# Sums of x in two tasks and two lanes, begun when the block's x is there

## The chip, the cores and the metric

The kernel runs on one core of a Trainium2 chip. The time is that of the device, in microseconds (us), from one execution of the program; three executions of the kernel before gave 2139.3, 2142.45 and 2143.07, a median of 2142.45. The profile is that of one more execution.

## What is computed

Three layers follow one another, all in 32 bits:

```
attention (4 batches, 8 heads, 576 tokens, head 64, 128 random features):
    phi(x) = exp(x @ omega.T - |x|^2/2 - max) / sqrt(128)
    out    = phi(q) (phi(k)^T v) / (phi(q) sum(phi(k)) + 1e-6)       -> x [2304, 512]
first layer (8 experts, w1[e] 512 x 1024, w2[e] 1024 x 512):
    P = exp(x @ w_gate - max); 8 times: rows /= sums, columns /= sums, *= 2304/8
    x = sum over e of P[:, e] * (relu(x @ w1[e]) @ w2[e])
second layer (w_in 512 x 2048, w_out 2048 x 512):
    out = (h * sigmoid(1.702 h)) @ w_out,   h = x @ w_in
```

## The kernel before

**Tiles.** Every 32-bit operand of a matmul is split into a high part (`..h`) and a rest (`..l`), and each product is three matmuls: high times high, high times low, low times high. The 2304 tokens are three blocks of 768 (`j` = 0, 1, 2). A block's x lies transposed in `blk_h[j]` and `blk_l[j]`: 4 k tiles of 128 of the 512 inner elements by 768 tokens. The 1024 or 2048 middle columns go in chunks of 256. One **visit** of the loop in `moe` is one chunk with one block (in the first expert partly half a block); there are 128 of them, numbered from 0. A visit has an up part (x times the chunk of the first weight, into `hh`, `hl`) and a down part of 36 matmuls (tile `py`, L892), whose results VectorE adds to the accumulators.

**Two ways up.** The first expert and the first chunk of the second layer (`ch` is `(E, 0)`) use `up`: 48 matmuls a visit (tile `ph`, L713). All other visits use `up_fast`: the 2 x 2 product of halves (two k halves, two token halves) is made with seven products in place of eight, 42 matmuls (L805), at the price of sums of weights and of x. Visits 0 to 19 are the first expert, 0 to 15 for blocks 0 and 1 (most of them beside attention), 16 to 19 for block 2. Visit 20 is the first with `up_fast`, block 0; 21 is block 1, 22 block 2. Visits 104, 105 and 106 are chunk `(E, 0)` of the second layer; 107, 108 and 109 are its first with `up_fast`.

**The sums of x.** With X[kh][i] for k half kh and token half i, `up_fast` wants s1 = X01 + X11, s2 = s1 - X00, s3 = X00 - X01 (tiles `th`, `tl`, high and low, index 0, 1, 2) and s4 = X10 - s2, which is written over X01 itself. For each of the two k tiles of a half (`kk`), `x_sums` (L729) issues two operations on VectorE and seven on GpSimd (`tt`, L738; names `t` and `u`), four casts to the high part on ScalarE (L761, L767, L772, L781) and four rests on VectorE (`lo`, L743). It is one generator per block: kk = 0 is issued wholly before kk = 1, with one `t` and one `u` from the pool of two buffers `t2`. s4 stands at the end of each kk, since X01 may be overwritten only when the `up` visits of the block are past (`free`).

**What sets the order.** The program is recorded in the order in which this code runs, and each engine executes its own instructions in that order. After each piece of a visit the loop at L1092 adds an estimate of its TensorE time to `now`, and calls `background()` (L958), which runs one step of one generator: a begun `spare` (the doubling of the second layer's weights from 64 bits, `double_piece`, L531), else the first of the deque `urgent` (the sums), else a new `spare`. `pool_done` (L102) holds a step back until `now` has passed the estimate `pool` of GpSimd's end. Every third piece also runs a step of `gates`, the eight row and column divisions (`sinkhorn`, L478: VectorE, then a matmul `pc`, L508, that TensorE runs in its place). A block's sums go into `urgent` when no `up` visit of the first layer needs the block any more (L1056), or, for the second layer, at the end of visits 102 to 104 (L1058). Before an `up_fast` visit, L1028 looks whether the block's sums are all issued; if not, `hurry` issues the rest at once, ahead of the visit.

**Others on GpSimd.** GpSimd also makes the sums of the weights of a chunk (`make_sums`, L628) and the low parts of the next chunk's first weight (`split`, L579, tiles `g0l`, `g1l`, `g2l`), which the first visit of that chunk reads.

## Time and profile before

| | |
|---|---|
| median of three runs | 2142.45 us |
| the profiled execution | 2136.16 us, span 2133.7 us |
| TensorE (PE) busy | 2090.6 us, 98% of the span |
| VectorE (DVE) busy | 1409.1 us, 66% |
| ScalarE (ACT) busy | 798.7 us, 37% |
| GpSimd (POOL) busy | 482.6 us, 23% |
| mean granted TensorE clock | 0.993 of full speed |

The span runs from the first to the last instruction; 2.5 us of the profiled execution lie outside it. Attention lasts until about 308 us of the span, the first layer until about 1723, the second to the end. PE is matmuls, PEld weight loads. A wait counts only on the engine that others wait for, here nearly always TensorE.

### The profile page before, as it was taken

The numbers are of one execution on the slowest core, as the hardware profiler recorded it, in microseconds if no ns is written. First come the engines' busy times: TensorE is split into PE (matmuls) and PEld (weight loads), VectorE is DVE, ScalarE is ACT, GpSimd is POOL, SyncE is SP. The second block draws the span as 40 slices with busy tenths as digits, with TensorE's granted clock in tenths as the row PEclk, the third lists the DMA queues.
The fourth block names the chain that finished last, engine by engine and source line by source line (L and its number), as shares of the span: only waits on it lengthen the run. The fifth ranks groups of instructions, "written<-read, shape, count | busy, mean of one in ns | idle before, by whom it ended". The sixth has DMA issues, their size and how long they took to land.

```text
span 2133.7 us, 29280 instructions
## 1 busy us (share of the span) xinstructions
PE 2090.6 (98%) x11040; PEld 1894.8 (89%) x11040; DVE 1409.1 (66%) x2630; ACT 798.7 (37%) x1770; POOL 482.6 (23%) x505
## 2 busy tenths in 40 slices
PE   8999999989999999999999999999999998799999
PEld 8999978878989999899999989999998997799987
DVE  7666547767666766766667676766555666566676
ACT  7655543532333323223332322333232354343443
POOL 3212224522121112212211221222111035311110
PEclk9999999999999999999999999999999999899999
DMA  8333211111112111111111111111000000000002
GB/s 164 86 80 90 70 52 48 40 37 46 45 42 59 51 50 44 49 45 42 57 53 50 43 50 45 43 57 33 20 20 20 20 20 20 20 21 20 20 21 89
DMA packets 147965, 100.54 MB, mean 47 GB/s; under 512 B 63600, under 2 KB 125040, under 8 KB 147824
## 3 DMA queue, kind: packets, MB, share of 16 engines
q1 hardware_dynamic: 147824, 98.68, 16.6%
q8 instruction: 86, 1.41, 0.3%
q14 instruction: 55, 0.45, 0.1%
HBM read 85.54 MB, written 13.11 MB: 46 GB/s over the span
## 4 chain that ended last, share of the span: by engine, by line
PE 92%; DVE 4%; ACT 2%; POOL 1%; issue 1%; DMA 0%; SPq 0%; ACTq 0%; POOLq 0%; DVEq 0%
PE py L892 45%; PE le L805 15%; PE ri L805 10%; PE ph L713 6%; PE pc L805 5%; PE pd L805 5%; PE num L304 2%; PE kv L274 1%; POOL u L738 1%; PE xt L342 1%; PE pj L240 1%; PE pj L242 1%; PE pj L241 1%; PE qt L297 1%; PE pt L215 1%
## 5 line engine op out<-in xcount | busy, mean ns | idle before, releaser
L892 PE MATMUL py<-w,hh 128*128 128x512 f32 x2880 | 895.6, 392 | 0.6 <-ACT hh L676 0.6
L892 PEld LDWEIGHTS py<-w,hh 128*128 128x128 f32 x2880 | 533.3, 188 | 104.7 <-ACT hh L676 1.9
L892 PE MATMUL py<-w,hl 128*128 128x512 f32 x1440 | 563.5, 391 | 0.0
L909 DVE SCALAR_TENSOR_TENSOR a<-py,lg,a 128x512 f32<-128x512 f32 x504 | 367.0, 747 | 132.7 <-PE py L892 132.4
L892 PEld LDWEIGHTS py<-w,hl 128*128 128x128 f32 x1440 | 270.2, 188 | 58.2 <-DVE hl L684 0.9
L823 ACT COPY m<-le 128x384 f32<-128x384 f32 x105 | 50.3, 479 | 528.5 <-PE le L805 528.4
L579 POOL TENSOR_TENSOR g0l<-w,g0h 128x768 fp32r<-128x768 f32 (+1 forms) x52 | 86.9, 1671 | 698.3 <-ACT g0h L578 679.8
L563 POOL TENSOR_TENSOR tmp<-tmp 128x256 f32<-128x256 f32 x64 | 47.3, 739 | 636.4 <-DVE tmp L560 346.5
L816 DVE TENSOR_TENSOR pc<-pc,m 128x384 f32<-128x384 f32 x105 | 59.5, 566 | 140.1 <-PE pc L805 140.0
L628 POOL TENSOR_TENSOR w<-w 128x256 f32<-128x256 f32 x140 | 108.0, 792 | 41.1 <-DMA w<-scr_in 22.1
L579 DVE TENSOR_TENSOR w<-r,w 128x512 fp32r<-128x512 f32 x104 | 75.8, 742 | 50.9 <-ACT w L578 50.9
L686 DVE SCALAR_TENSOR_TENSOR hl<-pc,hh 128x384 fp32r<-128x384 f32 x84 | 46.8, 558 | 90.8 <-ACT hh L678 89.2
L578 ACT CAST w<-r 128x512 fp32r<-128x512 f32 x104 | 63.6, 629 | 115.2 <-PE py L892 114.7
L837 ACT COPY u<-le 128x384 f32<-128x384 f32 x105 | 50.5, 481 | 137.7 <-PE le L805 137.7
L260 ACT ACTIVATE feat<-pj,nb 128x128 f32<-128x128 f32 x272 | 73.9, 386 | 68.2 <-DVE nb L256 61.5
L913 DVE TENSOR_TENSOR o<-py,o 128x512 f32<-128x512 f32 x126 | 84.3, 686 | 22.4 <-PE py L892 22.2
L816 DVE TENSOR_TENSOR le<-le,m 128x384 f32<-128x384 f32 x105 | 59.3, 565 | 45.7 <-ACT m L857 45.7
L805 PE MATMUL le<-th,g1h 128*128 128x384 f32 x210 | 73.1, 348 | 12.9 <-ACT m L823 12.9
L805 PE MATMUL ri<-th,g0h 128*128 128x384 f32 x210 | 72.2, 344 | 9.6 <-ACT th L761 9.6
L678 ACT ACTIVATE hh<-ri 128x384 fp32r<-128x384 f32 x84 | 41.2, 491 | 91.6 <-DVE ri L816 91.6
L805 PE MATMUL le<-tl,g1h 128*128 128x384 f32 x210 | 72.4, 345 | 0.0
L805 PE MATMUL ri<-tl,g0h 128*128 128x384 f32 x210 | 72.1, 344 | 0.2 <-DVE tl L743 0.2
(252 smaller groups left out, 4561.6 us busy)
## 6 DMA issues: line engine op xcount, KB each, us to landing
w<-in_moe_w_dram SPq DMA_DIRECT2D x176, 128.0 KB, 2.4
r<-in_moe_w_dram SPq DMA_DIRECT2D x44, 512.0 KB, 3.7
raw<-in_moe_w_in_dram SPq DMA_DIRECT2D x32, 256.0 KB, 3.0
raw<-in_moe_w_out_dram SPq DMA_DIRECT2D x32, 256.0 KB, 2.9
k<-in_k_dram SPq DMA_DIRECT2D x16, 256.0 KB, 4.2
v<-in_v_dram SPq DMA_DIRECT2D x16, 256.0 KB, 4.8
q<-in_q_dram SPq DMA_DIRECT2D x16, 256.0 KB, 4.6
scr_in<-tmp SPq DMA_DIRECT2D x32, 128.0 KB, 1.9
```

Of the source, the lines that this page charges most:

```text
L260: nc.scalar.activation(f[:, h, :], pvs[h // 4][:, h % 4, :], AF.Exp, bias=nb[:, h : h + 1])
L578: nc.scalar.copy(hi, r)
L579: eng.tensor_tensor(out=lo, in0=r, in1=hi.bitcast(F32), op=ALU.subtract)
L628: nc.gpsimd.tensor_tensor(out=r[:, o], in0=r[:, x], in1=r[:, y], op=ALU.subtract)
L713: nc.tensor.matmul(o, w[kk][a], x[j][:, 2 * kh + kk, th * Q : (th + 1) * Q], start=m == 0, stop=m == 3 * NK - 1,)
L805: nc.tensor.matmul(o, a[kk][x], b[kk][y], start=start and kk == 0 and n == 0, stop=kk == 1 and n == 2, skip_group_check=True,)
L816: nc.vector.tensor_tensor(out=o, in0=a, in1=b, op=ALU.add)
L823: nc.scalar.copy(m1, le)
L837: nc.scalar.copy(u2, le)
L892: nc.tensor.matmul(py[t], a[:, c], w, start=f == halves[0] and m == 0, stop=f == halves[1] and m == 2,)
L909: nc.vector.scalar_tensor_tensor(out=o, in0=py, scalar=pg[:, n, e : e + 1], in1=o, op0=ALU.mult, op1=ALU.add)
L913: nc.vector.tensor_tensor(out=o, in0=py, in1=o, op=ALU.add)
```

## The change

The sums become two tasks for each block, and each task is two generators, one for each `kk`. `x_sums` makes s1, s3 and s2 (five operations on GpSimd for each kk), and `x_sum4` makes s4 from X10 and the finished s2, high and low part apart (three on GpSimd). `urgent` becomes a list of two deques (lanes), and `background` runs a step of both. Lane 1 takes its `t` and `u` from two more buffers, `t3`, in the phase's own pool. `x_sums` of all three blocks goes into the lanes when attention is over, `x_sum4` of blocks 0 and 1 behind it, that of block 2 at the end of visit 19, and those of the second layer at the end of visits 104, 105 and 106. `free` and `used` go. In the order, L735 and L739 of the new program are what L738 and L743 were.

```diff
--- before.py
+++ after.py
@@ -726,7 +726,22 @@
 
     sums_done = set()
 
-    def x_sums(key, xh, xl, free):
+    def new_temp(lane, name):
+        if lane == 0:
+            return tm2([P, Q], F32, name)
+        return ph["sb"].tile([P, Q], F32, tag="t3", bufs=2, name=name)
+
+    def pool_tt(out, a, b, op, behind=0.0):
+        nc.gpsimd.tensor_tensor(out=out, in0=a, in1=b, op=op)
+        pool_busy(1.1, behind)
+
+    def dve_tt(out, a, b, op):
+        nc.vector.tensor_tensor(out=out, in0=a, in1=b, op=op)
+
+    def quads(x, kk):
+        return [[x[:, 2 * kh + kk, i * Q : (i + 1) * Q] for i in range(2)] for kh in range(2)]
+
+    def x_sums(key, xh, xl):
 
 
         j = key[1]
@@ -734,54 +749,56 @@
         xs_h[j] = th = sb.tile([P, 3, 2, Q], F32R, tag=f"th{j}", name=f"th{j}")
         xs_l[j] = tl = sb.tile([P, 3, 2, Q], F32R, tag=f"tl{j}", name=f"tl{j}")
 
-        def tt(out, a, b, op, eng=nc.gpsimd, behind=0.0):
-            eng.tensor_tensor(out=out, in0=a, in1=b, op=op)
-            if eng is nc.gpsimd:
-                pool_busy(1.1, behind)
-
-        def lo(out, t, hi):
-            nc.vector.tensor_tensor(out=out, in0=t, in1=hi.bitcast(F32), op=ALU.subtract)
-
-        for kk in range(2):
-
-            def quad(t, kh, i):
-                return t[:, 2 * kh + kk, i * Q : (i + 1) * Q]
-
-            bh, bl = (
-                [[quad(x, a, b).bitcast(F32) for b in range(2)] for a in range(2)] for x in (xh, xl)
-            )
-            t, u = tm2([P, Q], F32, "t"), tm2([P, Q], F32, "u")
-            tt(t, bh[0][1], bl[0][1], ALU.add, nc.vector)
-            yield
-            tt(u, bh[1][1], t, ALU.add, behind=1.5)
-            tt(u, u, bl[1][1], ALU.add)
-            yield
-            tt(t, bh[0][0], t, ALU.subtract, nc.vector)
+        def task(kk):
+            (h00, h01), (_, h11) = ([y.bitcast(F32) for y in r] for r in quads(xh, kk))
+            (l00, l01), (_, l11) = ([y.bitcast(F32) for y in r] for r in quads(xl, kk))
+            t, u = new_temp(kk, "t"), new_temp(kk, "u")
+            dve_tt(t, h01, l01, ALU.add)
+            yield
+            pool_tt(u, h11, t, ALU.add, 1.0)
+            pool_tt(u, u, l11, ALU.add)
+            yield
             yield from pool_done()
             nc.scalar.copy(th[:, 0, kk], u)
-            tt(t, t, bl[0][0], ALU.add, behind=1.0)
-            yield
-            lo(tl[:, 0, kk], u, th[:, 0, kk])
-            tt(u, u, bh[0][0], ALU.subtract, behind=1.5)
+            dve_tt(t, h00, t, ALU.subtract)
+            yield
+            dve_tt(tl[:, 0, kk], u, th[:, 0, kk].bitcast(F32), ALU.subtract)
+            pool_tt(t, t, l00, ALU.add)
+            yield
+            pool_tt(u, u, h00, ALU.subtract, 1.0)
+            pool_tt(u, u, l00, ALU.subtract)
             yield from pool_done()
             nc.scalar.copy(th[:, 2, kk], t)
-            tt(u, u, bl[0][0], ALU.subtract)
-            yield
-            lo(tl[:, 2, kk], t, th[:, 2, kk])
+            nc.scalar.copy(th[:, 1, kk], u)
+            yield
+            dve_tt(tl[:, 2, kk], t, th[:, 2, kk].bitcast(F32), ALU.subtract)
+            yield
+            dve_tt(tl[:, 1, kk], u, th[:, 1, kk].bitcast(F32), ALU.subtract)
+
+        return [task(kk) for kk in range(2)]
+
+    def x_sum4(key, xh, xl):
+
+        j = key[1]
+
+        def task(kk):
+            h, l = quads(xh, kk), quads(xl, kk)
+            u = new_temp(kk, "u")
+            pool_tt(u, h[1][0].bitcast(F32), xs_h[j][:, 1, kk].bitcast(F32), ALU.subtract, 1.0)
+            pool_tt(u, u, xs_l[j][:, 1, kk].bitcast(F32), ALU.subtract)
+            pool_tt(u, u, l[1][0].bitcast(F32), ALU.add)
+            yield
             yield from pool_done()
-            nc.scalar.copy(th[:, 1, kk], u)
-            yield
-            lo(tl[:, 1, kk], u, th[:, 1, kk])
-            while not free():
-                yield
-            tt(u, bh[1][0], u, ALU.subtract, behind=1.5)
-            tt(u, u, bl[1][0], ALU.add)
-            yield
-            yield from pool_done()
-            nc.scalar.copy(quad(xh, 0, 1), u)
-            yield
-            lo(quad(xl, 0, 1), u, quad(xh, 0, 1))
-        sums_done.add(key)
+            nc.scalar.copy(h[0][1], u)
+            yield
+            dve_tt(l[0][1], u, h[0][1].bitcast(F32), ALU.subtract)
+            sums_done.add((key, kk))
+
+        return [task(kk) for kk in range(2)]
+
+    def sum_up(tasks):
+        for lane, t in zip(urgent, tasks):
+            lane.append(t)
 
     def up_fast(cur, j, prep):
 
@@ -945,7 +962,7 @@
     seen = set()
 
     gates = sinkhorn()
-    urgent = deque()
+    urgent = [deque(), deque()]
     spare = deque()
 
     def run(q):
@@ -959,8 +976,10 @@
 
         if begun():
             run(spare)
-        elif urgent:
-            run(urgent)
+        elif any(urgent):
+            for lane in urgent:
+                if lane:
+                    run(lane)
         elif spare and may_start[0]:
             run(spare)
 
@@ -1025,12 +1044,12 @@
 
             key = (ch[0] // E, j)
             if cur.fast:
-                while key not in sums_done:
-                    hurry(urgent)
+                for kk, lane in enumerate(urgent):
+                    while (key, kk) not in sums_done:
+                        hurry(lane)
                 h = yield from up_fast(cur, j, prep)
             else:
                 h = yield from up(cur, j, halves, prep)
-            used.add((ch, j))
             if v == 0 and nx:
                 nx.load2()
             if nx and left <= 2:
@@ -1053,13 +1072,11 @@
                 yield dt
             for _ in side or ():
                 pass
-            if idx < n_first and all(x[1] != j for x in visits[idx + 1 : n_first]):
-                urgent.append(x_sums(key, blk_h[j], blk_l[j], lambda: True))
+            if idx == n_first - 1 or ch == (E, 0):
+                sum_up(x_sum4(key, blk_h[j], blk_l[j]))
             if n_exp - 2 <= idx <= n_exp:
                 i = idx - n_exp + 2
-                urgent.append(x_sums((1, i), *nblk[i], lambda i=i: ((E, 0), i) in used))
-
-    used = set()
+                sum_up(x_sums((1, i), *nblk[i]))
 
     with tc.manual_schedule():
         setup()
@@ -1088,6 +1105,10 @@
         enter_phase("exp")
         ready.update((j, th) for j in range(NB) for th in range(2))
         spare.extend(double_pieces())
+        for j in range(NB):
+            sum_up(x_sums((0, j), blk_h[j], blk_l[j]))
+            if j < 2:
+                sum_up(x_sum4((0, j), blk_h[j], blk_l[j]))
         pool[0] = now[0]
         for cnt, dt in enumerate(m):
             now[0] += dt
```

**The end of attention.** GpSimd's order where the first sums of block 0 meet the low parts of the weights for visit 15. Before (`u`, `t` are the temporaries, `xh_695` and `xl_696` block 0):

```order
L738 TENSOR_TENSOR u_3905<-xh_695,t_3904 128x384
L738 TENSOR_TENSOR u_3905<-u_3905,xl_696 128x384
L579 TENSOR_TENSOR g0l_3920<-w_3789,g0h_3919 128x2x256
L579 TENSOR_TENSOR g1l_3924<-w_3789,g1h_3923 128x256
L579 TENSOR_TENSOR g2l_3928<-w_3789,g2h_3927 128x256
L738 TENSOR_TENSOR t_3904<-t_3904,xl_696 128x384
L738 TENSOR_TENSOR u_3905<-u_3905,xh_695 128x384
L738 TENSOR_TENSOR u_3905<-u_3905,xl_696 128x384
```

The same place in the new program (`u_3909` is lane 0, `u_3912` lane 1):

```order
L735 TENSOR_TENSOR u_3909<-xh_695,t_3908 128x384
L735 TENSOR_TENSOR u_3909<-u_3909,xl_696 128x384
L735 TENSOR_TENSOR u_3912<-xh_695,t_3911 128x384
L735 TENSOR_TENSOR u_3912<-u_3912,xl_696 128x384
L579 TENSOR_TENSOR g0l_3929<-w_3789,g0h_3928 128x2x256
L579 TENSOR_TENSOR g1l_3933<-w_3789,g1h_3932 128x256
L579 TENSOR_TENSOR g2l_3937<-w_3789,g2h_3936 128x256
L735 TENSOR_TENSOR t_3908<-t_3908,xl_696 128x384
L735 TENSOR_TENSOR t_3911<-t_3911,xl_696 128x384
```

Four sums instead of two now stand ahead of the three `L579`.

**The end of block 2's sums in the first layer.** GpSimd before, between the weight sums (`L628`) and the splits for the chunk of visit 23, that is from visit 21 to visit 22's down part (`xh_2984`, `xl_2985` are block 2):

```order
L628 TENSOR_TENSOR w_4745<-w_4745 128x256 x4
L738 TENSOR_TENSOR u_4908<-xh_2984,u_4908 128x384
L738 TENSOR_TENSOR u_4908<-u_4908,xl_2985 128x384
L738 TENSOR_TENSOR u_5081<-xh_2984,t_5080 128x384
L738 TENSOR_TENSOR u_5081<-u_5081,xl_2985 128x384
L738 TENSOR_TENSOR t_5080<-t_5080,xl_2985 128x384
L738 TENSOR_TENSOR u_5081<-u_5081,xh_2984 128x384
L738 TENSOR_TENSOR u_5081<-u_5081,xl_2985 128x384
L738 TENSOR_TENSOR u_5081<-xh_2984,u_5081 128x384
L738 TENSOR_TENSOR u_5081<-u_5081,xl_2985 128x384
L579 TENSOR_TENSOR g0l_5198<-w_4745,g0h_5197 128x768
L579 TENSOR_TENSOR g1l_5202<-w_4745,g1h_5201 128x512
```

GpSimd in the new program, where block 2's s4 of both lanes stands (`th2`, `tl2` hold s2), and the next weight sums:

```order
L735 TENSOR_TENSOR u_4853<-xh_2984,th2_3889 128x384
L735 TENSOR_TENSOR u_4853<-u_4853,tl2_3890 128x384
L735 TENSOR_TENSOR u_4853<-u_4853,xl_2985 128x384
L735 TENSOR_TENSOR u_4857<-xh_2984,th2_3889 128x384
L735 TENSOR_TENSOR u_4857<-u_4857,tl2_3890 128x384
L735 TENSOR_TENSOR u_4857<-u_4857,xl_2985 128x384
L563 TENSOR_TENSOR tmp64_5027<-tmp64_5027 128x256
L628 TENSOR_TENSOR w_4788<-w_4788 128x256 x4
L563 TENSOR_TENSOR tmp64_5128<-tmp64_5128 128x256
L579 TENSOR_TENSOR g0l_5232<-w_4788,g0h_5231 128x768
L579 TENSOR_TENSOR g1l_5236<-w_4788,g1h_5235 128x512
L579 TENSOR_TENSOR g2l_5240<-w_4788,g2h_5239 128x512
```

Before, the nine rows of block 2's second half of sums stand behind the weight sums made in visit 21. Now the last six stand ahead of them, and work of `double_piece` (`L563`) follows. In the second layer it is alike: the last sums of block 2 stand ahead of visit 109's `up_fast` by more than a visit, and no step is issued by `hurry` anywhere.

**The divisions.** VectorE between the second and the third reading of `cs` by TensorE (`ct`, `rc`, `lg`, `r`, `rr`, `cs` belong to `sinkhorn`). Before:

```order
L686 SCALAR_TENSOR_TENSOR hl_4131<-ph_4117,hh_4130 128x384
L743 TENSOR_TENSOR xl_696<-u_3905,xh_695 128x384
L738 TENSOR_TENSOR t_4141<-xh_695,xl_696 128x384
L511 TENSOR_SCALAR ct_4150<-pc_4148 128x8
L512 RECIPROCAL rc_4151<-ct_4150 128x8
L513 SCALAR_TENSOR_TENSOR lg_79<-lg_79,rc_4151 128x144
L738 TENSOR_TENSOR t_4141<-xh_695,t_4141 128x384
L496 TENSOR_REDUCE r_4187<-lg_79 128x18
L497 TENSOR_SCALAR r_4187<-r_4187 128x18
L498 RECIPROCAL rr_4188<-r_4187 128x18
L499 TENSOR_TENSOR lg_79<-lg_79,rr_4188 128x144
L503 TENSOR_REDUCE cs_4193<-lg_79 128x8
```

The same stretch in the new program (`tl0_3886` are rests of block 0's sums):

```order
L686 SCALAR_TENSOR_TENSOR hl_4145<-ph_4131,hh_4144 128x384
L739 TENSOR_TENSOR tl0_3886<-u_3909,th0_3885 128x384
L739 TENSOR_TENSOR tl0_3886<-t_3911,th0_3885 128x384
L739 TENSOR_TENSOR tl0_3886<-u_3912,th0_3885 128x384
L511 TENSOR_SCALAR ct_4166<-pc_4164 128x8
L512 RECIPROCAL rc_4167<-ct_4166 128x8
L513 SCALAR_TENSOR_TENSOR lg_79<-lg_79,rc_4167 128x144
L496 TENSOR_REDUCE r_4204<-lg_79 128x18
L497 TENSOR_SCALAR r_4204<-r_4204 128x18
L498 RECIPROCAL rr_4205<-r_4204 128x18
L499 TENSOR_TENSOR lg_79<-lg_79,rr_4205 128x144
L503 TENSOR_REDUCE cs_4210<-lg_79 128x8
```

Three rests stand ahead of `ct` where a rest and a sum stood (and one more rest ahead of the `L686`), and the sum behind `L513` is gone.

## Rows read from the trace of the kernel before

**Rows 1.** The page: busy us, share of the span, instructions

```profile
PE 2090.6 (98%) x11040; PEld 1894.8 (89%) x11040; DVE 1409.1 (66%) x2630; ACT 798.7 (37%) x1770; POOL 482.6 (23%) x505
```

**Rows 2.** Waits of TensorE: waiter, releaser: us in total, times, longest

```profile
PE le L805 <- ACT m L823: 12.9, 3, 5.0
PE ri L805 <- ACT th L761: 9.6, 3, 7.0
PE pc L508 <- DVE cs L503: 4.5, 5, 1.9
...
PE ph L713 <- POOL g2l L579: 3.0, 1, 3.0
```

**Rows 3.** Chain of work, first layer: start us, us, what

```profile
422.02 6.86 PE py L892 x30
...
439.20 1.00 POOL u L738
...
441.16 2.29 PE le L805 x6
...
446.94 8.20 PE py L892 x36
455.14 1.06 PE le L805 x6
...
462.52 7.52 PE py L892 x33
```

**Rows 4.** Timeline of TensorE, second layer, visit 107's first down matmuls

```profile
1783.33 0.63 PE L892 MATMUL py<-w,hh 128*128 128x512 f32 x2
```

**Rows 5.** Chain of work, second layer, visits 108 to 110

```profile
1807.88 6.86 PE py L892 x30
...
1838.61 8.20 PE py L892 x36
...
1854.20 8.20 PE py L892 x36
```

**Rows 6.** Windows: stretch, its length, busy us per engine, granted clock, DMA

```profile
309.00:398.65 89.65, 82.13 (x413) 72.25 (x413) 64.16 (x138) 31.05 (x65) 43.75 (x43) 1.00 0.16 48
1704.85:1775.60 70.75, 70.75 (x379) 64.13 (x379) 42.80 (x69) 40.69 (x80) 26.58 (x26) 1.00 0.05 16
431.00:447.00 16.00, 10.10 (x39) 8.89 (x38) 6.59 (x11) 4.17 (x9) 7.24 (x7) 0.79 0.00 1
1816.00:1838.60 22.60, 11.67 (x44) 10.50 (x43) 9.78 (x18) 5.64 (x12) 9.48 (x9) 0.62 0.00 0
```

**Rows 7.** Timeline of GpSimd: sums and splits ahead of visits 15, 17, 104

```profile
309.96 1.02 POOL L738 TENSOR_TENSOR u<-xh,t 128x384 f32<-128x384 f32 x1 [11.04 <-DVE t L738]
...
312.40 1.29 POOL L579 TENSOR_TENSOR g0l<-w,g0h 128x512 fp32r<-128x512 f32 x1
...
314.79 1.16 POOL L579 TENSOR_TENSOR g2l<-w,g2h 128x256 fp32r<-128x256 f32 x1
...
339.50 1.28 POOL L579 TENSOR_TENSOR g0l<-w,g0h 128x512 fp32r<-128x512 f32 x1
...
1716.11 1.29 POOL L579 TENSOR_TENSOR g0l<-w,g0h 128x512 fp32r<-128x512 f32 x1
```

**Rows 8.** Timeline of TensorE: first matmuls of visits 15, 17 and 104

```profile
316.00 0.44 PE L713 MATMUL ph<-xh,g2l 128*128 128x384 f32 x1 [2.99 <-POOL g2l L579]
...
344.70 0.34 PE L713 MATMUL ph<-xh,g0l 128*128 128x384 f32 x1
...
1723.24 0.33 PE L713 MATMUL ph<-yh,g0l 128*128 128x384 f32 x1
```

**Rows 9.** Instructions of single lines: ns min/median/max

```profile
L499 DVE TENSOR_TENSOR lg<-lg,rr x8: 307/679/1036, 324.4 to 376.7; 128x144 f32<-128x144 f32 x8
L738 POOL TENSOR_TENSOR u<-u,xl x18: 990/1016/1429, 311.1 to 439.2; 128x384 f32<-128x384 f32 x18
L738 DVE TENSOR_TENSOR t<-xh,t x6: 547/554/559, 311.0 to 431.8; 128x384 f32<-128x384 f32 x6
```

## The prediction

> **What bounds the kernel now.** I read the page first: TensorE is busy for 98% of the span, GpSimd for 23% [rows 1]. So nothing is to be won but TensorE's own idle time, and nothing is lost elsewhere unless TensorE comes to wait for it. The waits of TensorE come next [rows 2]: the two largest, 12.9 us and 9.6 us, are `le` for ScalarE's `m` and `ri` for ScalarE's `th`, three times each. `th` is a high part of a sum of x; `m` is no sum, but the copy stands on ScalarE behind the last cast of a sum. In the chain of waits the steps between one visit's down part and the next are a ladder from VectorE to GpSimd to ScalarE and back, with `u` from L738 as its longest rungs; the last ends at 440.20 [rows 3]. These are the steps that `hurry` issues at once ahead of visits 22, 108 and 109: each needs the one before it, and TensorE has nothing else to do.
>
> What a ladder costs is read from the starts of the down parts, not from the idle time alone. Undisturbed, two follow each other after 15.58 us (446.94 to 462.52); around visit 22 it is 24.92 us (422.02 to 446.94), so 9.34 us are lost [rows 3]. In the second layer visit 107's down part begins at 1783.33 [rows 4] and visit 109's at 1838.61 [rows 5]: 55.28 us for two visits, where two undisturbed ones take 2 x 15.59 (1838.61 to 1854.20), 31.18. There 24.10 us are lost. The windows say what the idle time leaves out: the granted clock is 0.79 of full speed from 431 to 447 and 0.62 from 1816 to 1838.6 [rows 6], so part of each loss is matmuls at 1.2 GHz after the wait: six `le` take 2.29 us at 441.16 and 1.06 us at 455.14 [rows 3]. Both parts go if the wait goes.
>
> **The change part by part.** *The waits at visits 22, 108 and 109.* In the new order block 2's last sums stand ahead of visit 22 by more than a visit, and the same holds for all blocks of the second layer; nothing is left to `hurry`. For this to help, the engines must also have the time. The first layer's sums now begin at once at 309 us and need 48 operations on GpSimd instead of 42 (eight for each `kk` instead of seven), 6 x 1.02 us more [rows 9]; of the 89.65 us up to 398.65 GpSimd was busy for 43.75, and of the 70.75 us from visit 103 to 107 for 26.58 [rows 6]. So 46 and 44 us are idle, and what moves into them is block 2's sums in the first layer, 16 operations or 16 us, and in the second at most 34 operations of blocks 1 and 2, 35 us. ScalarE has as many casts as before and VectorE as many operations, only earlier. So I take the whole gain: 9.34 + 24.10 = 33.4 us. What is late next at these visits is the loads and splits of the weights, which in undisturbed visits cost nothing (15.58 us each). Bounds: 33.4 at most, nothing if the lanes stay late.
>
> *The splits for visit 15.* Here GpSimd's order puts four sums, not two, ahead of the three L579. In the trace the two begin at 309.96 and the first split at 312.40, 2.44 us later; the splits run until 315.95, and TensorE, which wants `g2l` first, waits 2.99 us for it and starts at 316.00 [rows 7, 8]. Two more sums in front move that start by another 2.4 us. The second lane's `t` is one VectorE operation of 0.55 us [rows 9], done while GpSimd is at lane 0. Ends: 3.0 us gained if the wait vanished, 4.9 lost if the sums took as long as the longest seen, 1.43 us, and the other lane's `t` came late. I take 2.4 us lost.
>
> *TensorE's clock there.* After 2.99 us of waiting it still ran at full speed (0.34 to 0.44 us a matmul, rows 8); after the waits of visit 22 it ran at half [rows 3]. The wait becomes 5.4 us. Ends: nothing, and 1.2 us as for the six `le`. I take 1.2 us: the three waits of `le` were at most 5.0 us each [rows 2], and the new one is longer.
>
> *The divisions.* TensorE waits 4.5 us in five of the eight `pc` matmuls for VectorE's `cs` [rows 2]. The sums' operations on VectorE stand between one reading of `cs` and the next; counted in the order, those five stretches hold one, one and two more than before, then two fewer, then two more: four more, each 0.55 us [rows 9]. 2.2 us lost. The ends: 4.5 us gained if all of these waits went; 5.9 lost if, besides, each of the five L499 took the longest time seen, 1036 ns, in place of the shortest, 307 ns [rows 9] (5 x 0.73 = 3.6 more).
> L499 itself shows how far apart two executions of one instruction lie, 307 and 1036 ns. The Trainium skill (SBUF — State Buffer, "Who interferes with whom") has a reason: a VectorE instruction with both inputs in SBUF and a GpSimd instruction that reads SBUF exclude each other, and whoever comes second waits for the other's end. It speaks against this change, which puts more sums on GpSimd beside the divisions; the trace agrees with it, since the 729 ns between the two are less than one `u` of 1016 ns [rows 9]. By it at its worst the sum would be 3.6 us higher, 2118.5 instead of 2115.
>
> *The other splits.* Ahead of visit 17 six sums stand before the splits where two stood: four more, 4.1 us. The first split began at 339.50 and took 1.28 us, and TensorE read `g0l` at 344.70: 3.9 us of slack, to which come the 2.4 us by which TensorE itself is later [rows 7, 8]. Ahead of visit 104 four more sums as well; the split's end at 1717.40 was 5.8 us before its reader at 1723.24 [rows 7, 8]. I take nothing for these and for visits 18, 19, 20 and 107; a lane that starts a microsecond late would cost up to 1 us each, 6 us in all.
>
> *The rest.* Two more buffers, the order of ScalarE's casts (each held back until GpSimd's end by estimate), and the doubling of weights, which begins a visit earlier, lie beside TensorE's work: nothing. The cover is ScalarE's load of 31.05 us in 89.65 and 40.69 in 70.75 [rows 6]; a cast issued too early would hold ScalarE, and so `hh`, which is in the 6 us above.
>
> The sum: 33.4 - 2.4 - 1.2 - 2.2 = 27.6 us. From the profiled execution's 2136.16 us that gives 2108.6. The median of the runs lies 6.3 us above it, so I forecast 2115 us.
>
> **The rivals.**
> *Nothing is given back.* GpSimd and VectorE have slack, and visit 15's wait or some of the divisions' could be absorbed: 2142.45 - 33.4 = 2109 us, with visit 15's wait gone too 2106. For it speaks that VectorE is idle for 25 of the 89.65 us; against it, the four sums in one row ahead of L579.
> *Half is given back at the splits.* If in visits 17 to 20, 104 and 107 GpSimd is late by 2 us each, 12 us, the gain is 15.6: 2127 us. For it speaks that up to six sums stand in a row where there were two; against it, the slack of 3.9 and 5.8 us.
> *Slower: the weight splits become the bound.* One mechanism, GpSimd's one queue: at the seven chunk starts from visit 15 to 107 TensorE waits for `g0l` behind four more sums. At the longest seen, 1.43 us [rows 9], that is 5.7 us each, 40 us, and with the 2.2 us of the divisions a loss of 8.8: 2151 us. It decides from 33.4 / 7 = 4.8 us a start. Against it speak the slack again and GpSimd's 46 idle us.
> *The change doesn't do what it says.* The sums stand early in the order, yet a lane could be held up on an engine (by its two buffers, or a cast behind other work) until the same visits: 2142 us. Against it, a whole visit, 15.6 us, lies between the last sum and visit 22.
>
> **How the numbers follow.** The forecast has 0.60, nothing given back 0.15, half given back 0.15, slower 0.05, no effect 0.05. 0.2% of the time, 4.3 us, is about what a measurement of this kernel can tell from no change; the first three are beyond it: faster 0.90, same 0.05, slower 0.05. The range takes the first two and most of the third, and the unknown ends of the splits (6 us) and of the divisions (3.6 us) on the upper side: 2106 to 2128.
>
> **What would show it.** In the new profile the down parts of visits 21 to 23 and 107 to 110 should follow each other after 15.6 us, the waits of `ri` for `th` and `le` for `m` should all but vanish, and the granted clock there be 1.00. TensorE's wait for `g2l` should be about 5.4 us instead of 3.0, those of `pc` for `cs` some 6 to 7 us instead of 4.5, and no wait for `g0l` over 1 us should appear. The prediction is wrong if a ladder of `u` still stands in the chain at visits 22, 108 or 109, or if waits for L579 at several chunk starts have taken its place.

## The result and the profile after

The changed kernel took 2116.95 us (median of four runs, 2113.8 to 2119.29), the kernel before 2142.28 in the same comparison: a ratio of 0.9887 with a 95% interval of 0.9872 to 0.9901. The forecast was 2115, the range 2106 to 2128. The profiled execution took 2119.29 us (span 2116.0), 16.9 below that of before.

The page of the changed kernel, its busy row: GpSimd and VectorE each do some more, TensorE 4.2 us less, against [rows 1].

```profile
PE 2086.4 (99%) x11040; PEld 1891.9 (89%) x11040; DVE 1419.0 (67%) x2630; ACT 797.3 (38%) x1770; POOL 500.7 (24%) x517
```

The waits of TensorE in the changed kernel (waiter, releaser: us in total, times, longest), the answer to [rows 2]:

```profile
PE pc L508 <- DVE cs L503: 7.9, 4, 2.4
PE ph L713 <- POOL g2l L579: 4.9, 1, 4.9
...
PE py L909 <- ACT hh L676: 1.8, 4, 1.2
...
PE le L822 <- ACT m L840: 1.0, 1, 1.0
```

`ri` for `th`, 9.6 us before, is gone from the list, and 12.9 us of `le` for `m` have become one wait of 1.0. In their place the two smaller waits of before have grown, `pc` from 4.5 to 7.9 and `ph` from 3.0 to 4.9.

The chain of waits, first layer, down parts of visits 20, 21 and 22 (start us, us, what), against [rows 3]; then the second layer's visits 106, 108 and 109, against [rows 5]:

```profile
419.15 8.20 PE py L909 x36
...
434.74 8.20 PE py L909 x36
...
450.32 8.20 PE py L909 x36
```

```profile
1771.04 8.22 PE py L909 x36
...
1793.18 4.74 PE py L909 x18
...
1805.30 8.20 PE py L909 x36
...
1820.89 8.20 PE py L909 x36
```

Visit 22 follows visit 21 after 15.58 us, as an undisturbed one does; all of the 9.34 us are back. From visit 108 on the second layer runs at 15.59 us too. Only visit 107 does not: its second half begins at 1793.18 behind a wait. From 106 to 109 it is 49.85 us. Before, visit 106 stood here in the chain:

```profile
1767.41 8.22 PE py L892 x36
```

From there to visit 109 [rows 5] it was 71.20 us: 21.35 us won.

Windows of the changed kernel (stretch, length, busy us per engine, granted clock, DMA), against [rows 6]:

```profile
316.00:330.00 14.00, 10.21 (x38) 9.47 (x39) 4.91 (x8) 2.21 (x5) 3.75 (x5) 0.76 0.25 77
348.00:356.00 8.00, 6.22 (x23) 5.39 (x24) 7.04 (x13) 2.40 (x6) 7.05 (x8) 0.79 0.16 48
419.15:450.32 31.17, 31.17 (x158) 28.28 (x157) 21.89 (x43) 15.62 (x30) 5.57 (x8) 1.00 0.09 29
...
1805.30:1836.47 31.17, 31.17 (x158) 28.28 (x157) 21.82 (x39) 14.29 (x29) 6.42 (x6) 1.00 0.11 34
```

Where the clock had been 0.79 and 0.62 of full speed, it is 1.00. Two stretches behind the end of attention have it below 1.00 instead. The next two views show what stood ahead of them. GpSimd's timeline ahead of visit 15, against [rows 7], and TensorE's, against [rows 8]:

```profile
311.86 1.26 POOL L735 TENSOR_TENSOR u<-xh,t 128x384 f32<-128x384 f32 x1 [10.99 <-DVE t L739]
...
314.17 1.01 POOL L735 TENSOR_TENSOR u<-xh,t 128x384 f32<-128x384 f32 x1
...
316.21 1.71 POOL L579 TENSOR_TENSOR g0l<-w,g0h 128x512 fp32r<-128x512 f32 x1
...
319.01 0.72 POOL L579 TENSOR_TENSOR g2l<-w,g2h 128x256 fp32r<-128x256 f32 x1
```

```profile
319.79 0.69 PE L713 MATMUL ph<-xh,g2l 128*128 128x384 f32 x1 [4.88 <-POOL g2l L579]
...
332.86 0.39 PE L508 MATMUL pc<-cs,ones 128*128 128x8 f32 x2 [1.44 <-DVE cs L503]
...
349.78 0.60 PE L508 MATMUL pc<-cs,ones 128*128 128x8 f32 x2 [2.37 <-DVE cs L503]
...
367.90 0.39 PE L508 MATMUL pc<-cs,ones 128*128 128x8 f32 x2 [1.97 <-DVE cs L503]
...
388.94 0.39 PE L508 MATMUL pc<-cs,ones 128*128 128x8 f32 x2 [2.13 <-DVE cs L503]
```

Four sums, from 311.86 on, stand ahead of `g0l`, as the order had said, and TensorE waits 4.88 us for `g2l`. Then it runs at half speed for a while. The chain has the first group of 23 matmuls, the changed kernel's first and then that of before:

```profile
319.79 7.04 PE ph L713 x23
```

```profile
316.00 4.28 PE ph L713 x23
```

That is 2.76 us more for the same matmuls. The correction product `pc` at 349.78 has waited 2.37 us and is itself slow (0.60 us for 0.39). There are eight products `pc`, and the first, third, fifth and eighth wait now. Before, five of them waited, the first, third, fifth, sixth and eighth:

```profile
325.74 0.39 PE L508 MATMUL pc<-cs,ones 128*128 128x8 f32 x2 [0.88 <-DVE cs L503]
...
341.45 0.39 PE L508 MATMUL pc<-cs,ones 128*128 128x8 f32 x2 [1.16 <-DVE cs L503]
...
356.22 0.39 PE L508 MATMUL pc<-cs,ones 128*128 128x8 f32 x2 [0.20 <-DVE cs L503]
362.70 0.39 PE L508 MATMUL pc<-cs,ones 128*128 128x8 f32 x2 [1.88 <-DVE cs L503]
...
377.67 0.39 PE L508 MATMUL pc<-cs,ones 128*128 128x8 f32 x2 [0.41 <-DVE cs L503]
```

In visit 107 the timeline of TensorE in the changed kernel has these two waits:

```profile
1785.39 0.45 PE L822 MATMUL le<-th,g2h 128*128 128x384 f32 x1 [0.87 <-ACT u L854]
...
1793.18 0.73 PE L909 MATMUL py<-w,hh 128*128 128x512 f32 x2 [1.21 <-ACT hh L676]
```

### The profile page after: what moved, and what is told of

The parts are those of the page before. It is cut to its first block, busy times and chain, and to the rows that moved or that the text cites. A ratio compares the mean times of both kernels' runs of the same rounds, so it can differ in the third digit from the quotient of the medians.

```text
span 2116.0 us, 29301 instructions
## 1 busy us (share of the span) xinstructions
PE 2086.4 (99%) x11040; PEld 1891.9 (89%) x11040; DVE 1419.0 (67%) x2630; ACT 797.3 (38%) x1770; POOL 500.7 (24%) x517
## 4 chain that ended last, share of the span: by engine, by line
PE 94%; DVE 3%; ACT 2%; issue 0%; POOL 0%; DMA 0%; SPq 0%; ACTq 0%; POOLq 0%; DVEq 0%
PE py L909 45%; PE le L822 15%; PE ri L822 10%; PE ph L713 6%; PE pc L822 5%; PE pd L822 5%; PE num L304 2%; PE kv L274 1%; PE xt L342 1%; PE pt L215 1%; PE qt L297 1%; PE pj L240 1%; PE pj L242 1%; PE pj L241 1%; DVE mx L244 1%
## 5 line engine op out<-in xcount | busy, mean ns | idle before, releaser
L579 POOL TENSOR_TENSOR g0l<-w,g0h 128x768 fp32r<-128x768 f32 (+1 forms) x52 | 87.1, 1675 | 724.8 <-ACT g0h L578 706.2
L563 POOL TENSOR_TENSOR tmp<-tmp 128x256 f32<-128x256 f32 x64 | 47.3, 738 | 637.3 <-DVE tmp L560 347.4
L628 POOL TENSOR_TENSOR w<-w 128x256 f32<-128x256 f32 x140 | 109.6, 804 | 44.8 <-DMA w<-scr_in 22.3
L579 DVE TENSOR_TENSOR w<-r,w 128x512 fp32r<-128x512 f32 x104 | 78.8, 771 | 52.3 <-ACT w L578 52.2
L686 DVE SCALAR_TENSOR_TENSOR hl<-pc,hh 128x384 fp32r<-128x384 f32 x84 | 46.8, 557 | 90.1 <-ACT hh L678 88.4
L822 PE MATMUL le<-th,g2h 128*128 128x384 f32 x210 | 71.5, 340 | 0.9 <-ACT u L854 0.9
L874 ACT COPY m<-pd 128x384 f32<-128x384 f32 x105 | 49.9, 475 | 57.3 <-PE pd L822 57.2
```

What stands on the lines that cost most here:

```text
L579: eng.tensor_tensor(out=lo, in0=r, in1=hi.bitcast(F32), op=ALU.subtract)
L628: nc.gpsimd.tensor_tensor(out=r[:, o], in0=r[:, x], in1=r[:, y], op=ALU.subtract)
L822: nc.tensor.matmul(o, a[kk][x], b[kk][y], start=start and kk == 0 and n == 0, stop=kk == 1 and n == 2, skip_group_check=True,)
```

## The experiments

Ten kernels ran. The first four are one comparison (before: 2137.72 us), the next four a second (2138.24), the last two a third (2140.75). The changed kernel is the reference of each edit; `...` stands for lines of it that are left out.

**The changed kernel again**, with no edit.

> The changed kernel again, beside the others of this comparison. Theory: 2115 to 2119 us, some 25 us less than before, with TensorE's waits as in its first profile: for the split of visit 15 4.9 us, for the divisions 7.9 us, none at visits 22, 108 and 109. Rival (the first profile caught an odd execution): these waits differ by more than 2 us.

2117.92 us (2113.34 to 2119.34), ratio 0.9896 [0.9879, 0.9912]; TensorE's waits for `cs`, `g2l`, `hh`, `m` and `u` are those above to the tenth. It is 19.8 us below its own before, not 25.3: medians of before lie up to 4.6 us apart between comparisons, so small steps below are read within one comparison or from the starts of visits.

**New sums in the second layer alone.**

```diff
...
-            if idx == n_first - 1 or ch == (E, 0):
+            if idx < n_first and all(x[1] != j for x in visits[idx + 1 : n_first]):
+                urgent[0].append(x_sums_old(key, blk_h[j], blk_l[j], lambda: True))
+            if ch == (E, 0):
                 sum_up(x_sum4(key, blk_h[j], blk_l[j]))
...
-        for j in range(NB):
-            sum_up(x_sums((0, j), blk_h[j], blk_l[j]))
-            if j < 2:
-                sum_up(x_sum4((0, j), blk_h[j], blk_l[j]))
```

> The first layer's sums are those of the kernel before (one generator a block, old starts), the second layer's those of the change. Theory (the whole net gain is the second layer's, because what the first layer gains at visit 22, 9.3 us, it gives back at visit 15, in the divisions and in matmuls at half clock, some 11 us): within 3 us of the changed kernel, 2113 to 2119 us, with a wait of about 3 us for the split of visit 15 and 4.5 us for the divisions, and the wait at visit 22 there again. Rival (both layers give their gain, as the prediction's sum had it, 9.3 less 5.8 in the first layer): 3 to 4 us slower than the changed kernel, about 2120 us.

(`x_sums_old` is `x_sums` of before.) 2116.81 us, ratio 0.9901 [0.9883, 0.9919], beside 2117.92. `pc` waits 4.5 us again and `ph` for `g2l` 3.0, as before the change, and visit 22 has its loss back: 423.94 to 448.84, 24.90 us. So in the first layer the change wins 9.3 us at visit 22 and pays them out again, about, at visits 15 to 20: as a whole the gain is the second layer's.

**The lanes held until visit 14's splits are recorded.**

```diff
+    hold = [True]
...
-        elif any(urgent):
+        elif any(urgent) and not hold[0]:
...
+                    if idx == 14:
+                        hold[0] = False
```

> As the changed kernel, but the lanes are run only from the point on at which the splits for visit 15 have been issued in visit 14, so that no sum stands ahead of them. Theory (the four sums ahead cost a wait of 4.9 us and, through the clock, about 2.8 us of slower matmuls): TensorE does not wait for that split, its clock stays at full speed there, and the time falls by 6 to 8 us against the changed kernel, to about 2110 us. Rival 1 (the split is late for another reason, its ScalarE cast or weights): the wait stays at 3 us or more. Rival 2 (the time comes back in the sums, which begin later): the wait goes and the time stays within 2 us.

2108.77 us, ratio 0.9858 [0.9843, 0.9873], 9.2 below the changed kernel in the same comparison, more than the 6 to 8 expected. Nothing waits for `g2l`; `pc` waits 9.1 us. Visit 22's down part begins at 441.98 where the changed kernel run beside it has 449.74: 7.8 us, about the wait of 4.9 and the 2.8 of half-clock matmuls behind it. The two traces differ elsewhere too, by amounts that partly cancel: the granted clock from 290 to 310 is 1.00 here and 0.91 beside it, and `pc` waits 1.2 us longer here. Of the wait 3.0 us stood in the kernel before too.

**The old start points in the first layer**, tasks and lanes as in the change (block 2 behind visit 19).

```diff
...
-            if idx == n_first - 1 or ch == (E, 0):
+            if idx < n_first and all(x[1] != j for x in visits[idx + 1 : n_first]):
...
+                late_sums.append(both) if None not in late_sums else both()
+            if ch == (E, 0):
                 sum_up(x_sum4(key, blk_h[j], blk_l[j]))
...
-        for j in range(NB):
-            sum_up(x_sums((0, j), blk_h[j], blk_l[j]))
-            if j < 2:
-                sum_up(x_sum4((0, j), blk_h[j], blk_l[j]))
+        for t in late_sums:
+            t()
```

> The changed kernel's two tasks and two lanes, but in the first layer each block's sums go into the lanes where the kernel before put them: block 1 after visit 15, block 2 after visit 19. Theory (what removes the wait at visit 22 is the two lanes, not the early start): no wait at visit 22, the time within 2 us of the changed kernel. Rival (the early start is what removes it): a ladder of sums at visit 22 again and 5 to 9 us more.

2114.01 us, ratio 0.9881 [0.9866, 0.9897]. A block's sums enter the lanes only when no `up` visit needs the block any more. Visit 22 has no wait (down parts at 429.28 and 444.87) although its sums begin no earlier than before. What removes the ladder is two lanes with their own temporaries, not the early start, which brought nothing: this kernel is 3.9 us below the changed one beside it, though their runs overlap (2111.32 to 2116.71 and 2113.34 to 2119.34).

**Both tasks in one lane**, two temporaries, early start kept.

```diff
-        if lane == 0:
-            return tm2([P, Q], F32, name)
-        return ph["sb"].tile([P, Q], F32, tag="t3", bufs=2, name=name)
+        return tm2([P, Q], F32, name)
...
-        for lane, t in zip(urgent, tasks):
-            lane.append(t)
+        urgent[0].extend(tasks)
...
```

> Both tasks of a block go into one lane, one behind the other, and only the two old temporaries are used; the three sums, the fourth from the second and the new start points stay. Theory (the second lane, with temporaries of its own, is what ends the k tile 1 in time): in the second layer the rest of a task is again recorded in one piece ahead of the matmuls that read it, so the waits of the correction matmuls on the splits (th) and of the gate on its temporary return at visits 107 to 109, some 15 to 24 us of them; at visit 22 too, since one lane of four times six steps begun early is drained one step at a time. Time 2130 to 2145 us, 15 to 28 us above the changed kernel. Rival (the earlier start and the shorter sums do it, two lanes are an extra): no wait over 2 us at visits 22 and 107 to 109, time 2112 to 2120 us.

2140.22 us, ratio 1.0009 [1.0000, 1.0018]: nothing of the gain is left. The chain of this kernel around visit 22:

```profile
422.69 8.22 PE py L906 x36
...
438.19 2.17 POOL u L733 x2
...
446.94 2.29 PE le L819 x6
...
452.95 8.20 PE py L906 x36
```

The ladder of `u` on GpSimd is back, longer than in [rows 3] (30.26 us from visit 21 to 22 where it was 24.92), with `le` at half speed behind it. In the second layer visits 106 to 109 take 70.1 us (1773.27 to 1843.41), nearly before's 71.2. Early start and the new tasks without the second lane are worth nothing. In the second layer the change begins the sums behind the same visits as before (102 to 104), so there the gain can't be the start's. Lane and temporaries went together here; which of the two is needed was not tried apart.

**Hold and old starts together.**

```diff
+        elif any(urgent) and not hold[0]:
...
+                def both(key=key, j=j):
+                    sum_up(x_sums(key, blk_h[j], blk_l[j]))
+                    sum_up(x_sum4(key, blk_h[j], blk_l[j]))
+
+                late_sums.append(both) if None not in late_sums else both()
...
```

> The hold of the lanes until visit 14's splits and the old start points of the first layer's blocks together (block 2 behind visit 19, not 17), tasks and lanes as in the changed kernel. Theory (the two take their gain from different places: the hold the wait on g2l and its half-clock stretch at visit 15, the old starts only the few sums that stand in visits 17 to 19): no wait on g2l over 3.1 us, waits of the correction products on the divisions 6 to 9 us, time 2104 to 2109 us, 8 to 13 us below the changed kernel. Rival (both act on one backlog of VectorE, so they don't add): 2108 to 2112 us, the same as the hold alone.

2108.64 us, ratio 0.9866 [0.9850, 0.9883]: beside 2108.77 of the hold alone the time is the same, though before stood 0.5 us higher. The number lies in both ranges that were expected. By the theory the two add: 3.9 us of the old starts on top of the hold would give, by an estimate from these two runs, some 2105 us, which was not seen, so the rival is right on the time. Its reason, one backlog of VectorE, is not shown by this run. `pc` still waits 8.9 us, the longest 2.8.

**GpSimd fills instead of adding, first layer.** It tells whether `cs` is late because more of the sums' operations stand ahead of it on VectorE, or because these are held up by GpSimd.

```diff
-        nc.gpsimd.tensor_tensor(out=out, in0=a, in1=b, op=op)
+        if len(nblk):
+            nc.gpsimd.tensor_tensor(out=out, in0=a, in1=b, op=op)
+        else:
+            nc.gpsimd.memset(out, 0.0)
```

> In the first layer every sum on GpSimd is replaced by a fill of the same output tile on GpSimd, so that GpSimd writes the tile and reads nothing; the first layer's sums on GpSimd are left out of the computation. VectorE's and ScalarE's instructions stay the same in number and order. Theory (the waits on the divisions come from the count of VectorE's own sums ahead of them, 2 to 4 for each piece in place of 1 to 3): the waits on cs stay at 6 to 9 us in four pieces, the piece of VectorE work of line 499 keeps a mean above 0.60 us. Rival (VectorE's operations are held up by GpSimd's reads): line 499's mean falls towards its shortest, 0.31 us, the differences tl<-u fall from 0.63 to near 0.55 us, and the waits on cs fall to 4 to 5 us. A third outcome, a fall of both to the half, would say that each has a share.

2107.98 us in one run; `pc` waits 3.5 us with the same VectorE instructions in the same order that gave 7.9. Instructions of line 499 (ns min/median/max), the changed kernel first, then this one:

```profile
L499 DVE TENSOR_TENSOR lg<-lg,rr x8: 307/746/897, 331.6 to 387.7; 128x144 f32<-128x144 f32 x8
```

```profile
L499 DVE TENSOR_TENSOR lg<-lg,rr x8: 307/308/1158, 325.3 to 376.2; 128x144 f32<-128x144 f32 x8
```

The median falls from 746 to its shortest, 308 ns. The timeline of all engines in this kernel shows what decides:

```profile
336.21 2.78 POOL L738 MEMSET u<- 128x384 f32 x6 [7.86 <-DVE tl L742]
336.48 0.54 DVE L742 TENSOR_TENSOR tl<-u,th 128x384 fp32r<-128x384 f32 x1
...
338.31 0.31 DVE L513 SCALAR_TENSOR_TENSOR lg<-lg,rc 128x144 f32<-128x144 f32 x1
...
339.20 1.29 POOL L579 TENSOR_TENSOR g0l<-w,g0h 128x512 fp32r<-128x512 f32 x1 [0.22 <-ACT g0h L578]
339.50 1.16 DVE L499 TENSOR_TENSOR lg<-lg,rr 128x144 f32<-128x144 f32 x1
```

Beside the fills VectorE's operations take 0.54 and 0.31 us; beside `g0l`, which reads, line 499 takes 1.16 and ends 0.17 us after it. The Trainium skill (SBUF — State Buffer, "Who interferes with whom") says just this: a VectorE instruction with two SBUF inputs contends with a GpSimd instruction that reads SBUF, not with one that only writes it. The trace agrees. The rival held, and its waits are even below its 4 to 5 us. But the count, on which the prediction and this experiment's theory stood, is not without effect: at the two products that have two operations more ahead of them, the fifth and the eighth, `pc` waits 0.54 and 1.91 us here, where before had 0.20 and 0.41.

**One more step between `cs` and its reader**, with hold and old starts; the divisions are stepped behind every second group of matmuls, not every third.

```diff
                 out=cs, in_=pg.rearrange("p t e -> p e t"), op=ALU.add, axis=AX.X
             )
             yield
+            yield
             pc = ps("pc")
             nc.tensor.matmul(pc[:, 0:E], ones, cs, start=True, stop=True)
...
-            if cnt % 3 == 2:
+            if cnt % 2 == 1:
```

> The version with hold and old starts, and beside it one more step between a piece's division cs and the correction product that reads it, so that TensorE comes to that product one group of matmuls later; the division loop is stepped behind every second group of matmuls in place of every third to end at the same visit. Theory (TensorE waits because it comes to the product before VectorE has worked through the sums queued ahead of the division, 1.4 to 2.8 us each time): the waits on cs fall below 3 us in all, the half-clock stretches of 3.4 us behind them go, time 2098 to 2104 us. Rival (VectorE is behind by a whole backlog at this stage, so that a later product waits just as long, or the wait moves to the next reader): 5 to 9 us of waits stay on cs or on what follows it, time 2105 to 2112 us.

2100.60 us (2100.13 to 2101.32), ratio 0.9826 [0.9811, 0.9840]: 8.0 below the version without it and 37.6 below before, the fastest kernel here. `pc` waits 2.0 us, twice. Windows of the version without the step, then of this one:

```profile
360.00:380.00 20.00, 16.42 (x78) 14.54 (x76) 16.69 (x36) 5.69 (x13) 8.92 (x10) 0.91 0.18 52
```

```profile
360.00:380.00 20.00, 20.00 (x104) 17.87 (x103) 19.59 (x39) 7.30 (x15) 11.21 (x11) 1.00 0.14 45
```

TensorE goes from 16.42 busy us, part of it at half speed, to 20.00 of 20. The wait is 6.9 us shorter (8.9 to 2.0), and the clock's 0.09 of 20 us are another 1.8: together 8.7 where 8.0 were measured. VectorE's work is not less; its lateness no longer meets a reader. The theory held, the rival (a wait as long, later) did not.

**The later reader alone.** The two edits of the last diff on the changed kernel, without hold and old starts.

> The changed kernel with only the later correction product (one more step between a division cs and the product that reads it, the division loop stepped behind every second group of matmuls); no hold, the early starts kept. Theory (the waits on the divisions, 7.9 us and the half-clock stretches behind two of them, and the wait on g2l, 4.9 us with its half-clock stretch, are two separate losses): waits on cs below 3 us in all, the wait on g2l stays at 4 to 6 us, time 2107 to 2111 us, 6 to 10 us below the changed kernel and 6 to 10 us above the version with the hold as well. Rival (the divisions are late because the sums ahead of them began too early, so that without the hold the backlog outlasts one more group): 5 to 8 us of waits on cs stay, time 2113 to 2118 us.

2112.59 us, ratio 0.9871 [0.9855, 0.9888]. `pc` waits 2.5 us and `ph` for `g2l` 4.3, as the theory said, so the two losses are separate. The time is 1.6 us above the theory's 2111 and just below the rival's 2113: a new wait of 1.5 us for `g0l` eats part of it. Visit 22's down part is 5.1 us earlier than in the changed kernel (445.24 for 450.32). On the waits the theory is right, on the time it was too hopeful.

**Three fills for each sum, both layers**, so that GpSimd is busy as long as it is with sums.

```diff
-        nc.gpsimd.tensor_tensor(out=out, in0=a, in1=b, op=op)
+        for _ in range(3):
+            nc.gpsimd.memset(out, 0.0)
```

> In both layers every sum on GpSimd is replaced by three fills of the same output tile on GpSimd, about 1.26 us together by the 0.42 us of one in the last fill experiment, so that GpSimd is busy as long as with the sums (1.10 us) but reads nothing; the sums on GpSimd are left out of the computation. Theory (VectorE's operations are stretched by GpSimd's reads, and that is what makes the divisions late): line 499 keeps a mean below 0.50 us, the waits on cs stay at 3 to 5 us, and in the second layer the 0.9 us wait on the gate's temporary and the 1.2 us wait of py at visit 107 shrink to under half; the wait on g2l stays at 4 to 6 us, since it is GpSimd's own queue. Rival (what helped was that a fill is shorter than a sum, so that results came earlier): the waits on cs are back at 6 to 9 us and visit 107 keeps its 2 us. Third: the waits at visit 107 stay with short VectorE operations; then ScalarE's casts are their cause.

2107.52 us in one run. Line 499 has a mean of 401 ns, `pc` waits 2.8 us: GpSimd's reading, not the length of its work, is what stretches VectorE's operations and with them the waits for `cs`. Two expectations failed. `ph` does not wait for `g2l` here, since fills need no input from VectorE and begin earlier, and two waits for `g0l`, 3.2 us together, came instead. So this kernel says nothing on the wait at visit 15. In visit 107 the 1.2 us wait of `py` is gone, but `le` waits 2.0 us for the gate's `u`, where 0.9 was to shrink. Two views bear on this. First, VectorE in the changed kernel, two operations that lie before that `py`, beside a run of sums on GpSimd:

```profile
1789.95 1.34 DVE L739 TENSOR_TENSOR yl<-u,yh 128x384 fp32r<-128x384 f32 x1
1791.21 1.36 DVE L672 TENSOR_TENSOR m<-m,g 128x384 f32<-128x384 f32 x1
```

Then ScalarE ahead of `le`'s wait, the changed kernel and the one with three fills:

```profile
1784.07 0.51 ACT L772 CAST th<-u 128x384 fp32r<-128x384 f32 x1 [1.72 <-POOL u L735]
...
1784.87 0.47 ACT L854 COPY u<-le 128x384 f32<-128x384 f32 x1
```

```profile
1773.35 0.51 ACT L773 CAST th<-u 128x384 fp32r<-128x384 f32 x1 [2.23 <-POOL u L736]
...
1774.15 0.47 ACT L855 COPY u<-le 128x384 f32<-128x384 f32 x1
```

The two operations of 1.34 and 1.36 us (0.55 undisturbed) are stretched by GpSimd's reads, and without reads the wait of `py` goes. The wait of `le` is another thing: ScalarE stands in front of a cast whose sum GpSimd hasn't finished (1.72 us), and the gate and `u` are queued behind it. With three fills ScalarE waits 2.23 us there and `le` 2.0, although VectorE's operations are short: the third outcome, ScalarE's casts. Why this wait is longer than 1.72 us was not traced.

## Why the prediction was right, and where its terms were off

*The waits at visit 22.* 9.34 us were forecast and 9.34 came. The run with one lane and the one with old starts show that the lanes, with their temporaries, do it.

*The second layer.* 24.10 us were forecast, 21.35 came, and the run with the second layer alone, 20.9 us below its before, agrees. The 2.75 us short are visit 107's: 0.87 us of `le` behind ScalarE's cast, 1.21 us of `py` behind VectorE's stretched operations; the rest was not traced. (The 24.10 were counted from visit 107 on, the 21.35 from 106 on; the wait of `le` lies before 107's down part, in the stretch that was not counted.) The prediction had set "the order of ScalarE's casts" down as nothing, with its cost counted in the 6 us of the splits: the mechanism was named, the place was not.

*The splits for visit 15.* The wait grew by 1.89 us (2.99 to 4.88) where 2.4 was forecast from two sums of 1.2 us. The mechanism was right and the size near. (The bad end, 4.9 us, does not follow from the rows that it names: two sums at 1.43 us are 2.9.)

*TensorE's clock there.* 1.2 us were forecast from six `le` at half speed. The two rows of 23 matmuls show 2.8 us. In this trace the term was mis-sized by a factor of two: it took a row with six matmuls for the length of the slow stretch, and here more matmuls fell into it. But not all of it is the change's. The run with the second layer alone, whose first layer is that of before and whose wait for `g2l` is as long as before's (2.97 us), has this row in its chain:

```profile
316.35 5.82 PE ph L713 x23
```

That is 1.5 us more than before's 4.28 after the same wait, so before's trace had caught an execution in which the clock held.

*The divisions.* 2.2 us were forecast, 3.4 came (4.5 to 7.9), and another 1.7 us from the clock behind the 2.37 us wait at 349.78 (0.21 of the 8 us from 348 to 356), which had no term. The forecast's step was to count the operations ahead of `cs` and take 0.55 us for each. The count gave the places rightly. With one, one and two operations more ahead of the first, third and fifth product, the waits grew by 0.56, 1.21 and 1.77 us; with two fewer ahead of the sixth, its 1.88 us went; with two more ahead of the eighth, it grew by 1.72. The price was too low: 3.4 us for four operations are 0.85 each. The fills show why, as without GpSimd's reads the same operations leave `pc` only 3.5 us, less than the 4.5 of before. One operation takes longer beside a reading GpSimd: from 310 to 400 us `tl<-u` had a mean of 550 ns before (7 of them) and 784 after (9). The prediction had that cause in the upper end of its range, for line 499 alone. What the count costs where GpSimd only fills was not measured apart, since before was not run with fills.

*The other splits.* Forecast: nothing, with 6 us as the bound. Measured: one wait of 1.0 us at visit 20 (`le` for `m`). No wait for L579 came at any chunk start but visit 15, so the slower rival, GpSimd's queue as the bound at seven starts, is out, and so is the half given back.

The sum then: 9.34 + 21.35 won, 1.9 + 2.8 + 3.4 + 1.7 + 1.0 = 10.8 lost, 19.9 us net, where the forecast had 27.6. The two profiled spans differ by 17.7; most of the rest lies inside attention, where the program is the same. Windows there, of the changed kernel and of the one before:

```profile
290.00:310.00 20.00, 19.91 (x114) 16.90 (x114) 8.48 (x18) 5.24 (x11) 2.65 (x3) 0.91 0.19 57
```

```profile
290.00:310.00 20.00, 19.91 (x118) 16.23 (x118) 9.47 (x20) 6.82 (x15) 2.69 (x4) 1.00 0.18 60
```

The clock's 0.09 of 20 us cost 1.8 us in this execution. The changed kernel run again has 0.91 there too, while five edits that leave attention as it is (the second layer alone, the hold, the old starts, both, and one lane) have 1.00; what decides it was not found.

The medians differ by 25.3, nearer the forecast's 27.6 than the terms are: before's profiled execution lay 6.3 us below its median, that of after 2.3 above. So it is in part luck that the forecast came within 2 us of the median, since for the profiled execution it was 2108.6 and 2119.29 came. Step by step the forecast was 5.0 us too good in the first layer (10.8 against 5.8) and 2.75 in the second. The spread of the executions goes with their granted clock: the four of the changed kernel have mean clocks of 0.996, 0.996, 0.997 and 0.999 at 2119.29, 2118.15, 2115.76 and 2113.80 us.

## What to carry to other kernels

A chain of dependent steps over three engines is shortened by running two of them side by side with buffers of their own; beginning earlier brought nothing here, and it costs time where the extra instructions enter a queue that something on the critical path is about to read (keeping them out of GpSimd's queue at visit 15 was worth some 8 us here, 3.0 of which were a wait that stood there before). A short operation that TensorE waits for is best given a later reader, since how long it takes depends on what its neighbour engine does then, and one group of matmuls in between was worth 8 us.

## What the runs showed of the hardware

A fill on GpSimd of 128 x 384 took 0.42 us where a sum took 1.02 (the median of `u<-u,xl` in [rows 9]), and VectorE's operations beside the fills shown above were not stretched. Line 499 next to it ran in 0.31 us, next to a reading GpSimd instruction in up to 1.16.

The granted clock fell after waits that do not stand in order of length: after 4.88 us and 2.37 us in the changed kernel, not after the 2.99 us of [rows 8] nor after the 1.97 and 2.13 us of two other `pc` in the changed kernel. It fell in the run with the second layer alone after 2.97 us at the place of those 2.99. In attention TensorE waited 0.99 us for `x` in both kernels (289.21 before, 289.59 after), and from 290 to 295 the clock was 1.00 before and 0.67 after. Two versions waited 2.70 us at the same `pc` (at 324.4); their windows, the hold alone first, then hold and old starts:

```profile
310.00:330.00 20.00, 17.30 (x81) 15.34 (x80) 16.11 (x28) 4.83 (x11) 14.44 (x13) 0.91 0.18 54
```

```profile
310.00:330.00 20.00, 17.30 (x91) 15.38 (x90) 16.39 (x29) 5.64 (x14) 14.45 (x13) 1.00 0.18 54
```

The same wait left one at 0.91 and the other at full speed. What else decides was not tried; the fall behind 349.78 cost 1.7 us.
